# RWKV-7 recurrence with hashed experts: earlier loads for tiles 4 to 7, and the rounds of decays moved between two inversions

## The chip, the cores and the metric

The kernel runs on one core of one Trainium2 chip. The metric is the device time of one execution in microseconds (us), the median of several runs. The kernel before takes 647.45 us (three runs, 645.55 to 648.0); its profiled execution has a span of 645.1 us, and all times in the profile count from the start of that span.

The engines are named as the profile names them: PE is TensorE (matmul), PEld its weight loads, DVE is VectorE, ACT is ScalarE, POOL is GpSimd, SP is SyncE. SPq and POOLq are the queues of those two engines as issuers of DMA transfers.

## What is computed

Two blocks follow each other. The first is a recurrence with a state of 40 x 40 for each of 4 x 8 heads, over 768 steps; the second sends each of its 3072 output rows through one of 8 experts, chosen by a hash.

```python
# r, k, v, w, a, b: (4, 8, 768, 40)
for t in range(S):
    y[:, :, t] = einsum('bhd,bhde->bhe', rt, state)
    Sa = einsum('bhde,bhe->bhd', state, at)
    state = state * wt[:, :, None, :] - einsum('bhd,bhe->bhde', Sa, bt)
    state = state + einsum('bhd,bhe->bhde', vt, kt)
...
expert_idx = token_ids * 2654435761 % 8
for e in range(E):                       # x = y as rows (3072, 320)
    h = maximum(x[mask] @ w1[e], 0)
    out[mask] = h @ w2[e]
```

The kernel turns the recurrence into chunks of 64 steps. The products of the decays w over a chunk, called p and q, are multiplied into a, b, k and the output, so that within a chunk only matrices of 64 x 64 remain: one triangular matrix per head has to be inverted, and everything else is matmuls. Tile u is one chunk of two of the four batches (16 heads): 24 tiles in all.

## The kernel before

The kernel's instructions are not written in the order in which they run. Each piece of work registers itself with a "tick", and all pieces are recorded in the order of their ticks. Every engine then works through its own instructions strictly in that order. `order` settles ties. Tile u has its first part (scores) near tick u and its second part (the state's step) near tick u + 8. The names in STEPS give fractions of a tick.

```python
STEPS = ["r1","z","y","nc","x","at_t","x_t","s","u","sd","a","r_t","r0","rc"]

def at_tick(tick, step=None, order=0):
    if step is not None:
        tick += STEPS.index(step) / len(STEPS)
    ...                                  # plan.append((tick, order, n, f))
```

A "round" of decays makes p and q for two chunks, so for four tiles. It has three stages: five levels of products up a tree (`todo`), one matmul on PE that exchanges the halves' products (`f_ps`, from `own`), and two spreads down the tree that give p (in `pb`) and q (in `qb`).

```python
def decays(ri, t_w, t0, span, t_f, span_f=None, stores=None):
    @at_tick(t_w)                        # load w of the round into "wt"
    ...
    todo: 5 levels, pb and qb by DVE TENSOR_TENSOR (L368); the last is "own" (L365)
    then: 0  PE  f_ps <- own, partner                    (L384)
          1  DVE qb, ends <- f_ps, own                   (L391, L392)
          2  DVE reciprocal                              (L397)
          3  DVE pb spread, 4 levels                     (L377)
          4  DVE pb spread, last level; store p to DRAM  (L377, L339)
          5  DVE qb spread, 4 levels                     (L379)
          6  DVE qb spread, last level; store q to DRAM  (L379, L339)
          7  PE/ACT pend <- ends                         (L428, L433)
```

Round 0 is different: its p and q are turned into rows inside SBUF, and p's rows (`p_rows`) lie in a buffer of the tag "nu", which has one copy. They are written to DRAM as well, by one DMA (L408), since the output's multiplication needs them at tick 8.

```python
if ri == 0:
    x["p"] = p_rows = turned_rows(x["pb"][:],
        early.tile([P, 2*BLK*BLK], F32, tag="nu", name="p_rows"))
    at_tick_later.append(lambda: nc.sync.dma_start(pq_dram[ri][0]..., p_rows))   # L408
```

The same tag "nu" holds the working matrices of the inversion. One inversion serves a group of four tiles:

```python
def group_i(gi, t0, t1, t2):
    at t0 - 0.5:  nu = early.tile(..., tag="nu")           # POOL memset L591, L593
    at t0:        DVE transpose nu <- pk                   # L597
    t1 to t2:     30 steps of DVE multiply and add         # L615, L622
    at t2:        DVE transposes ut <- nu, twice           # L630, L631
...
for gi in range(NU // GRP):
    t0 = gi * GRP + GRP - 1 + t_a                          # t_a = 10/14
    group_i(gi, t0 + 0.05, t0 + 0.1, t0 + 3.4)
```

So group 0 takes its buffer at tick 3.26, is worked on from 3.76 and ends at 7.11; group 1 goes from 7.76 to 11.11, and so on. Between two inversions lie 0.65 ticks.

The inputs of a tile come by six DMAs from the SP queue (a, b and k, two halves each), into buffers `al` and `kb` of two copies each; for tiles 2 and 3 other buffers are lent (`x_t`, `mr`, `py`), which the second parts of the tiles need only from tick 8 on.

```python
@at_tick({0: -3.9, 1: -3.8, 2: -2.8, 3: -2.7}.get(u, max(u - 2.55, t_mult_of(u - 2) + 0.03)))
def _():
    kb_tag = {2: "x_t", 3: "mr"}.get(u)
    ...
    x["a"] = al = work.tile([P, DM], F32, tag="py" if kb_tag else "al", name="al")
    load(..., a, ...); load(..., b, ...); load(..., k, ...)          # L310

# DVE: at <- al, pl (L500) and z <- kb, ql (L507) at t_mult_of(u)
# PE: z_ps, t_ps, a_ps; ACT: z_t, at_t, pk, no; DVE: mk (L548)
```

`ql` and `pl` are q and p of the tile, loaded by the POOL queue (L468, L474). In the second part, PE runs in each tick r_ps, rc_ps, z_ps, y_ps, nc_ps, x_ps, t_ps, x_t_ps, s_ps, u_ps, sd_ps, a_ps; x_ps reads `ut` of the inversion, and u_ps needs both of its transposes.

Of the kernel before, what the change touches and what calls it, by code (L numbers as in the profile page):

```python
# [47 lines left out]
def kernel(  # L48
# [22 lines left out]
    NG = B // 2  # L71
# [100 lines left out]
# [4 lines that stand above are left out]
        def add(f):  # L176
            plan.append((round(tick, 4), order, len(plan), f))
            return f
        return add
# [53 lines left out]
    RN = P // (B * H * 2)  # L233
# [66 lines left out]
    def by_head(t, rows=slice(None)):  # L300
        return t[rows].rearrange("t (h e) -> t h e", h=H)
# [5 lines left out]
    def load(dst, src, b0, t0, crossed=False):  # L307

        for be in range(2):
            nc.sync.dma_start(dst(be, half(1 - be if crossed else be)),  # L310
                              src[b0 + be, :, t0:t0 + C, :].rearrange("h t e -> t h e"))
# [5 lines left out]
    def decays(ri, t_w, t0, span, t_f, span_f=None, stores=None):  # L317

        x = rounds[ri]
        todo, then = [], []  # L320
# [114 lines left out]
        if ri == 0:  # L435
            then = then[:3] + then[5:7] + then[3:5] + then[7:]
            at_tick_later = []
            at_tick(1.36)(lambda: [f() for f in at_tick_later])
        if stores is not None:
            at_tick(stores)(lambda: (store(0, x["pb"][:]), store(1, x["qb"][:])))  # L440
        for i, f in enumerate(todo):
            at_tick(t0 + span * i / len(todo), order=8)(f)
        for i, f in enumerate(then):
            at_tick(t_f[i] if isinstance(t_f, tuple) else t_f + span_f * i / len(then), order=8)(f)

    def of_batches(rows, b0, n):
        return rows[:, b0 * H:(b0 + n) * H, :].rearrange("t bh e -> t (bh e)")
# [3 lines left out]
    def t_mult_of(u):  # L451
        return u + LATE[u] - 0.1 if u in LATE else u - 0.6

    def tile_a(u):

        n, g = divmod(u, NG)
        ri, rn = divmod(n, RN)
# [6 lines left out]
        @at_tick({0: -2.2, 1: -2.19, 2: -0.9, 3: -0.8}.get(u, u - 1.7))  # L464
        def _():
            x["q"] = ql = work.tile([P, 2, DM], F32, tag="ql", name="ql")
            for be in range(2):
                nc.gpsimd.dma_start(ql[half(be)], of_batches(rows_of_chunk("q"), 2 * g, 2))  # L468
# [5 lines left out]
                nc.gpsimd.dma_start(pl[half(be)], of_batches(rows_of_chunk("p"), 2 * g + be, 1))  # L474


        @at_tick({0: -3.9, 1: -3.8, 2: -2.8, 3: -2.7}.get(u, max(u - 2.55, t_mult_of(u - 2) + 0.03)))
        def _():
            kb_tag = {2: "x_t", 3: "mr"}.get(u)
            if kb_tag:  # L480
                kb = work.tile([P, 2 * HP * P], F32, tag=kb_tag, name=f"kb_{kb_tag}", bufs=1)[:, 0:2 * DM].rearrange("p (b x) -> p b x", b=2)
            else:
                kb = work.tile([P, 2, DM], F32, tag="kb", name="kb")[:]
            x["kb"] = kb
            x["a"] = al = work.tile([P, DM], F32, tag="py" if kb_tag else "al", name="al")
            load(lambda be, rows: by_head(al, rows), a, 2 * g, n * C)

            load(lambda be, rows: by_head(kb[:, be], rows), b, 2 * g, n * C)
            load(lambda be, rows: by_head(kb[:, be], rows), k, 2 * g, n * C, crossed=True)
# [309 lines left out]
    t_a = STEPS.index("a") / len(STEPS)  # L799

    decays(0, -4.0, -3.0, 0.4, -2.5, 0.3)
    decays(1, -2.9, -1.9, 0.4, (-0.54, -0.53, -0.52, -0.5, -0.45, 0.75, 0.8, 0.85), stores=1.34)
    decays(2, 0.86, 2.7, 0.2, (3.0, 3.01, 3.02, 3.66, 3.67, 4.0, 4.3, 4.31))
    for ri in range(3, NR):
        t0 = ri * RN * NG - 5.0
        decays(ri, t0 - 2.0, t0 + 0.25, 1.0, t0 + 1.3, 1.1)
    for u in range(NU):
        tile_a(u)
        tile_s(u, u + LAG)
# [2 lines left out]
    for gi in range(NU // GRP):  # L812
        t0 = gi * GRP + GRP - 1 + t_a
# [500 lines left out]
```

## Time and profile before

| what | before |
|---|---|
| median of 3 runs | 647.45 us |
| span of the profiled execution | 645.1 us |
| first inversion, start of L597 to end of L631 | 46.98 to 88.82 us |
| recurrence with all engines, about | 89 to 396 us |
| experts, about | 396 to 645 us |
| PE / DVE / ACT / POOL busy, share of the span | 86% / 55% / 46% / 30% |
| DMA engines' busy share, 47 to 89 us | 0.96 |
| DMA engines' busy share, 131 to 280 us | 0.79 |

A line of a timeline gives the start, the duration (of several merged instructions where it ends in xN), the engine, the line of the kernel, the operation, and what it writes and reads. In brackets stand the engine's idle time just before it and what ended that. "issue" means that nothing in the profile explains the wait. A DMA instruction's own duration is that of its issue; the data land later.

### The profile page before, as it was taken

The page shows a single profiled execution, that of the slowest core. Times are in us where ns is not written, and L with a number is a line of the kernel's source. Part 1 is how long each engine was busy: PE and PEld are TensorE (multiplying, and loading weights), DVE is VectorE, ACT ScalarE, POOL GpSimd, SP SyncE. Part 2 cuts the span into 40 slices and gives each one's busy share as a digit, 9 for nine tenths or more (in the row PEclk, how much of TensorE's full clock was granted, in tenths as well). Part 3 has the DMA queues.
Part 4 walks back from the last instruction along what each step waited for, and adds up shares of the span by engine and source line. Part 5 has one row for each costly group of instructions (what it writes and reads, how often), then busy time and mean ns, then how long its engine had stood idle before and what let it go on. Part 6 is the DMA issues. An engine that isn't in the chain of part 4 may idle for free.

```text
span 645.1 us, 22962 instructions
## 1 busy us (share of the span) xinstructions
PE 556.3 (86%) x9866; PEld 422.7 (66%) x9866; DVE 351.6 (55%) x920; ACT 293.7 (46%) x695; POOL 195.8 (30%) x331
## 2 busy tenths in 40 slices
PE   0443568988999999999899998999999999999995
PEld 0332457877787878888788887666565646565552
DVE  6968679966977896797798553232021202203010
ACT  4162436757776677777767661113131304101100
POOL 0631341535333344432423321261313131230101
PEclk9975559989999999999999999999999999999999
DMA  8999988987797687842434613697333373220000
GB/s 160 198 197 178 163 154 143 190 144 137 149 184 148 129 169 149 153 97 45 103 60 116 155 53 97 223 290 248 110 102 113 105 264 103 66 96 20 30 12 25
DMA packets 195770, 85.13 MB, mean 132 GB/s; under 512 B 176718, under 2 KB 186191, under 8 KB 195664
## 3 DMA queue, kind: packets, MB, share of 16 engines
q1 hardware_dynamic: 184016, 45.59, 37.6%
q0 software_dynamic: 11456, 37.37, 20.1%
q8 instruction: 78, 1.28, 0.9%
q10 hardware_dynamic: 192, 0.66, 0.4%
q14 instruction: 28, 0.23, 0.1%
HBM read 66.54 MB, written 15.40 MB: 127 GB/s over the span
## 4 chain that ended last, share of the span: by engine, by line
PE 50%; issue 23%; DVE 10%; DMA 6%; SPq 5%; POOL 4%; ACT 2%; POOLq 0%; DVEq 0%; ACTq 0%
PE up_ps L1057 6%; PE dn_ps L1075 6%; PE y_ps L291 5%; PE s_ps L291 4%; PE rc_ps L291 3%; PE r_ps L291 3%; SPq L310 3%; PE x_t_ps L733 3%; PE a_ps L291 3%; PE t_ps L573 3%; PE sd_ps L793 3%; PE z_ps L521 2%; POOL out_dram L1080 2%; DVE mr L745 2%; PE nc_ps L291 2%
## 5 line engine op out<-in xcount | busy, mean ns | idle before, releaser
L1065 DVE TENSOR_SCALAR ht<-up_ps 128x416 f32<-128x416 f32 (+2 forms) x36 | 19.4, 543 | 165.2 <-PE up_ps L1062 163.7
L1075 PE MATMUL dn_ps<-w,ht 128*128 128x320 f32 x336 | 91.7, 433 | 0.0
L1057 PE MATMUL up_ps<-xt,w 128*128 128x416 f32 x224 | 81.3, 516 | 0.0
L1075 PEld LDWEIGHTS dn_ps<-w,ht 128*128 128x128 f32 x336 | 63.3, 190 | 25.5
L1080 POOL DMA_INDIRECT out_dram<-o,idx_all x26 | 26.1, 1004 | 165.4 <-ACT o L1079 164.3
L785 POOL DMA_DIRECT2D x_rows<-xs x44 | 23.2, 535 | 171.3 <-DVE xs L781 96.5
L1067 ACT ACTIVATE ht<-up_ps 128x416 f32<-128x416 f32 (+2 forms) x36 | 17.2, 478 | 107.5 <-PE up_ps L1062 107.4
L1057 PEld LDWEIGHTS up_ps<-xt,w 128*128 128x128 f32 x224 | 41.9, 190 | 36.8 <-issue 31.7
L615 DVE TENSOR_TENSOR outer<-nu 128x252 f32<-128x252 f32 (+8 forms) x180 | 63.4, 352 | 4.9
L622 DVE TENSOR_TENSOR nu<-nu,outer 128x252 f32<-128x252 f32 (+8 forms) x180 | 63.4, 352 | 4.3
L1079 ACT COPY o<-dn_ps 128x320 f32<-128x320 f32 x26 | 11.1, 425 | 92.4 <-PE dn_ps L1075 92.4
L521 PE MATMUL z_ps<-ident,z 128*104 128x128 f32 x192 | 31.2, 315 | 24.2 <-DVE z L507 21.4
L525 ACT COPY z_t<-z_ps 104x512 f32<-104x512 f32 x48 | 25.7, 588 | 47.4 <-PE z_ps L521 46.3
L521 PEld LDWEIGHTS z_ps<-ident,z 128*104 128x104 f32 x192 | 24.5, 150 | 27.1 <-issue 23.2
L468 POOL DMA_DIRECT2D ql<-q_rows x48 | 25.1, 531 | 48.4 <-DVE pb L377 15.4
L723 ACT COPY x<-nc_ps 64x320 f32<-64x320 f32 x48 | 20.1, 420 | 42.7 <-PE nc_ps L291 42.1
L745 DVE TENSOR_TENSOR mr<-rc_ps,after 128x1024 f32<-128x1024 f32 x24 | 29.3, 1220 | 13.6 <-PE rc_ps L291 13.6
L291 PE MATMUL rc_ps<-r_t,x_t 64*64 64x64 f32 x1536 | 30.1, 222 | 6.7 <-issue 6.0
L291 PE MATMUL a_ps<-at_t,z_t 64*64 64x64 f32 x1536 | 32.3, 241 | 3.6 <-ACT at_t L574 2.4
L291 PEld LDWEIGHTS a_ps<-at_t,z_t 64*64 64x64 f32 x1536 | 28.6, 152 | 8.1 <-ACT at_t L574 3.6
L548 DVE TENSOR_TENSOR mk<-a_ps,after 128x512 f32<-128x512 f32 x24 | 16.6, 690 | 28.9 <-ACT no L565 26.2
L291 PEld LDWEIGHTS rc_ps<-r_t,x_t 64*64 64x64 f32 x1536 | 25.7, 134 | 9.3 <-issue 6.1
(230 smaller groups left out, 1125.9 us busy)
## 6 DMA issues: line engine op xcount, KB each, us to landing
ql<-q_rows POOLq DMA_DIRECT2D x48, 160.0 KB, 4.3
w<-in_moe_w_dram SPq DMA_DIRECT2D x10, 640.0 KB, 7.6
w<-in_moe_w_dram SPq DMA_DIRECT2D x10, 512.0 KB, 4.3
al<-in_a_dram SPq DMA_DIRECT2D x48, 80.0 KB, 4.2
pl<-p_rows POOLq DMA_DIRECT2D x48, 80.0 KB, 4.5
r<-in_r_dram SPq DMA_DIRECT2D x48, 80.0 KB, 3.8
x<-in_v_dram SPq DMA_DIRECT2D x48, 80.0 KB, 3.7
py<-p_rows POOLq DMA_DIRECT2D x48, 80.0 KB, 4.8
```

Source lines behind the costliest of these rows:

```text
L291: nc.tensor.matmul(out_, lhsT=lhsT, rhs=rhs, start=start, stop=stop, skip_group_check=True)
L468: nc.gpsimd.dma_start(ql[half(be)], of_batches(rows_of_chunk("q"), 2 * g, 2))
L521: nc.tensor.transpose(p[0:R, be, hp * P:(hp + 1) * P], x["z"][:, be, hp, :], ident[:])
L525: nc.scalar.copy(t[0:R, be].rearrange("p h t -> p (h t)"), p[0:R, be])
L615: nc.vector.tensor_tensor(tv, paired(x["u"])[:, 0:full[1], j:j + 1, :].to_broadcast(full), paired(x["n"])[:, j // 2, j + 1:, j % 2].unsque ...
L622: nc.vector.tensor_tensor(o, o, x["t"][:, 0:n].rearrange("p (c i k) -> p c i k", c=full[1], k=2), op=OP.add)
L723: nc.scalar.copy(x["x"][half(be), be].rearrange("p (a q) (two e) -> p a (q two) e", a=2, two=2)[:, :, :, 0:D], p[half(be), :, 0:HP * D].re ...
L745: nc.vector.tensor_tensor(t[:].rearrange("p two h t -> p (two h) t"), p[:].rearrange("p two (h t) -> p (two h) t", t=C), after[:].unsqueez ...
L785: dma(x_of[2 * g + be, n * C:(n + 1) * C], xs[half(be), :])
L1057: nc.tensor.matmul(p[:], lhsT=w1[c][:, (f0 + i) * P:(f0 + i + 1) * P], rhs=xt[:, c, 0:n], start=(c == 0), stop=False)
L1075: nc.tensor.matmul(p[i * m:(i + 1) * m], lhsT=ht[:, f, c0:c0 + m], rhs=w2[f // (FP // 2)][:, f % (FP // 2), :], start=(f == 0), stop=(f == ...
L1080: st = nc.gpsimd.indirect_dma_start(out=out[:], out_offset=bass.IndirectOffsetOnAxis(ap=idx, axis=0), in_=o[0:m], in_offset=None, bounds_c ...
```

## The change

It does two things. The loads of tiles 4 to 7 get fixed, earlier ticks; tiles 6 and 7 borrow the buffers that tiles 2 and 3 had, so that they need not wait until tiles 4 and 5 have been used up. So that these loads come ahead of it, the DMA that writes round 0's p to DRAM is moved from tick 1.36 to 3.2. And rounds 3 to 5 of the decays, which before ran beside an inversion (round 3: products at ticks 7.25 to 8.25, the rest at 8.3 to 9.4), are put between two inversions (7.1 to 7.65), so that the inversion has VectorE for itself.

```diff
         if ri == 0:
             then = then[:3] + then[5:7] + then[3:5] + then[7:]
             at_tick_later = []
-            at_tick(1.36)(lambda: [f() for f in at_tick_later])
+            at_tick(3.2)(lambda: [f() for f in at_tick_later])
...
-            at_tick(t_f[i] if isinstance(t_f, tuple) else t_f + span_f * i / len(then), order=8)(f)
+            at_tick(t_f + span_f * i / len(then) if span_f else t_f[i], order=8)(f)
...
-        @at_tick({0: -3.9, 1: -3.8, 2: -2.8, 3: -2.7}.get(u, max(u - 2.55, t_mult_of(u - 2) + 0.03)))
-        def _():
-            kb_tag = {2: "x_t", 3: "mr"}.get(u)
+        @at_tick({0: -3.9, 1: -3.8, 2: -2.8, 3: -2.7, 4: 0.9, 5: 1.5, 6: 2.0, 7: 2.5}.get(u, max(u - 2.55, t_mult_of(u - 2) + 0.03)))
+        def _():
+            kb_tag = {2: "x_t", 3: "mr", 6: "x_t", 7: "mr"}.get(u)
...
     for ri in range(3, NR):
-        t0 = ri * RN * NG - 5.0
-        decays(ri, t0 - 2.0, t0 + 0.25, 1.0, t0 + 1.3, 1.1)
+        t0 = ri * RN * NG - 4.9
+        decays(ri, t0 - 2.1, t0, 0.12, [t0 + f for f in (0.13, 0.2, 0.21, 0.25, 0.35, 0.42, 0.5, 0.55)])
```

Before, the loads of tiles 4, 5, 6 and 7 stood at ticks 1.45, 2.45, 4.38 and 5.23. No arithmetic is added or removed.

## The prediction

> **What bounds the kernel now.** I read the busy table by stretches first. Up to 89 us PE is less than half busy (17.4 of the 42 us from 47 to 89) while DVE has 33.0 of 42 and the DMA engines a share of 0.96; from 131 to 280 us PE has 136.8 of 149. So the start is set by DVE and DMA, the recurrence by PE, and the change touches both. The experts after 396 us have nothing to do with it and only shift.
>
> Then the order in which the SP queue issues, because the change is mostly about that order:
>
> ```profile
> 19.04 1.99 SPq L310 DMA_DIRECT2D kb_mr<-in_k_dram  x2
> 30.11 4.20 SPq L339 DMA_DIRECT2D p_rows<-pb  x4
> 34.71 4.63 SPq L339 DMA_DIRECT2D q_rows<-qb  x4
> 39.39 1.71 SPq L408 DMA_DIRECT2D p_rows<-p_rows  x1
> 41.15 1.67 SPq L310 DMA_DIRECT2D al<-in_a_dram  x2
> ...
> 50.28 1.57 SPq L310 DMA_DIRECT2D kb<-in_k_dram  x2
> ```
>
> The queue stands still from 21.0 to 30.1 us behind the stores of round 1. The write of round 0's p (L408) follows the stores at once, and tiles 4 and 5 come only then (41.15 to 51.85 us).
>
> Who needs L408 is seen on POOL, and what follows on DVE:
>
> ```profile
> 44.63 0.95 POOL L591 MEMSET nu<- 128x1024 f32 x1 [1.22 <-DMA p_rows<-p_rows]
> ```
>
> ```profile
> 46.98 1.25 DVE L597 STREAM_TRANSPOSE nu<-pk 128x1024 f32<-128x1024 f32 x1 [1.21 <-ACT pk L564]
> ...
> 78.85 0.49 DVE L500 SCALAR_TENSOR_TENSOR at<-al,pl 128x320 f32<-128x320 f32 x1 [3.26 <-DMA al<-in_a_dram]
> 81.31 0.83 DVE L507 TENSOR_TENSOR z<-kb,ql 128x640 f32<-128x640 f32 x1 [1.97 <-DMA kb<-in_k_dram]
> ...
> 86.45 1.25 DVE L630 STREAM_TRANSPOSE ut<-nu 128x1024 f32<-128x1024 f32 x1
> 87.62 1.20 DVE L631 STREAM_TRANSPOSE ut<-nu 128x1024 f32<-128x1024 f32 x1
> ```
>
> The inversion cannot take the "nu" buffer before L408 has read round 0's p out of it: it landed 5.24 us after its issue (44.63 - 39.39). Here that just does not matter, as L597 waits until 46.98 for something else. From there DVE runs to 88.82 with 6.9 us idle in all: 5.23 us for the inputs of tile 7 (the two lines in the middle; this is what the change is after) and 1.66 us in two waits for ACT.
>
> PE's lines show what waits for the transposes, and the recurrence's gaps:
>
> ```profile
> 87.75 1.06 PE L291 MATMUL x_ps<-ut,no 32*32 32x32 f32 x32 [3.54 <-DVE ut L630]
> ...
> 90.61 1.06 PE L291 MATMUL u_ps<-um,xi 32*32 32x32 f32 x32 [0.75 <-ACT um L652]
> ...
> 136.05 0.45 PE L291 MATMUL rc_ps<-r_t,x_t 64*64 64x64 f32 x11 [2.26 <-issue]
> ```
>
> From 88 to 270 us PE waits only 1.8 us for DVE (twice y_ps for mr: 1.0 and 0.8), but 12.7 us for "issue". These gaps come once in about 380 matmuls, at places where the work has no boundary, such as after 53 of 64 rc_ps matmuls. No DVE work that moves away can remove them.
>
> **What the Trainium skill says.** "DMA: Bandwidth & Descriptors", Issuing engines are not separate DMA queues: transfers of all issuers run on the same 16 engines and interleave. The trace agrees: SP is idle from 21 to 30 us, yet the DMA share is 0.95 there, from POOL's transfers and the backlog. "Perfetto Trace Analysis", DMA Instruction — HWDGE: a DMA's reported window ends when its issue ends, the movement is outside. So L408's 1.71 us are not its cost; the 5.24 us until the memset are. "TensorE: Matmul & The Clock Gate", What's actually happening: after an idle window of about 3.4 us the array falls to half clock. The trace has half clock from 50 to 90 us, and after the 2.26 us gap above the next z_ps takes 1.95 us where it takes 1.08 in other ticks: PE waits that I add may cost more than their length. "Runtime: NRT & Kernel Launch", Instruction fetch mechanics: each engine's instructions are refilled in blocks of 256 by DMA and mostly hidden. 380 matmuls with their weight loads are 760 instructions, about three blocks, so I take the "issue" gaps for refills that the loaded DMA engines delay; the profile only suggests this, and here they are not hidden.
>
> **The change, part by part.** (1) The first inversion's start. In the changed program's SP order, tile 4's loads come before round 1's stores; tiles 5, 6, 7 follow the stores, and L408 only after them. Tile 4's buffers come free when DVE has done `at` of tile 0 (25.95 + 0.5), so its six loads go into the idle stretch: at the 0.67 us each that 12.25 to 16.28 shows for six, 26.5 to 30.5 us. Stores: 9.2 us as now (30.11 to 39.34), to 39.7. Eighteen loads: twelve took 8.8 us at 12.25 to 21.03 (0.73 each) and 10.7 us at 41.15 to 51.85 (0.89 each), so 13.2 to 16.0 us; I take 14.6, to 54.3. L408 lands 5.24 us later, at 59.5. L597 writes the same buffer and waits for the same DMA, so it starts near 59.5 instead of 46.98: +12.5 us. In DVE's order nothing of tiles 4 to 7 is ahead of L597, so DVE cannot fill that time.
>
> (2) From L597 on. The 5.23 us of waits for inputs vanish: -5.2. The first two products of round 3 (0.48 us each, 0.8 together by their starts) now stand ahead of L630: +0.8. L631 so ends at 88.8 + 12.5 - 5.2 + 0.8 = 96.9 instead of 88.8: **+8.1 us**.
>
> (3) Round 3 at the first x_ps. In the new PE order f_ps (from `own`) stands ahead of x_ps. DVE must first finish both transposes, then six products and `own` (0.32 + 0.32, 0.24 + 0.23, 0.19 + 0.19, 0.19; about 1.5 us by starts). f_ps takes 0.65, so x_ps begins about 2.2 us after L631. Before, u_ps began 1.8 us after L631; now x_ps 1.06, xi 0.74 and um 0.95 must come in between, so 4.9 us: **+3.1 us**.
>
> (4) Rounds 4 and 5, ticks 11.2 and 15.2: the same order, f_ps ahead of x_ps. From the end of rc_ps PE has r_ps 0.7, z_ps 1.0, y_ps 1.75, nc_ps 0.6 = 4.05 us until it wants f_ps. DVE has from there: mr 1.2, three steps 0.65, two products 0.8, two transposes 2.4, xs 0.4, the other products and `own` 1.25 = 6.7 us. PE waits 2.65 us in each round where it waited for nothing before: **+5.3 us**, or less where an "issue" gap falls into the same stretch.
>
> (5) What is given back: DVE no longer has 6 us of decays inside an inversion, so at most the two waits for mr, **-1.8 us**; the delayed start lets SP get ahead, so loads in front of the recurrence (the 5.25 us wait for ql at 90.95) meet less traffic: about **-1**; and gaps that coincide with (4): about **-1**.
>
> Sum: 8.1 + 3.1 + 5.3 - 1.8 - 2 = 12.7 us; 647.45 + 12.7 = 660. Two terms ((3) and (4)) rest on chains that may have slack which I do not see, so I put it at 659.
>
> **Rivals.** *A: the loads win.* If L408 lands early, the start is only freed of its waits: -5.2 us, and with the relief of DVE about -7, so 640 to 643. For it: DVE's 5.2 us are real. Against it: L408 stands behind 18 loads in one queue, and even at the quickest rate seen (0.65 us a load) it is issued at 51.4 and lands at 56.7, still 9.7 us late. *B: the DVE crowding is hidden.* If PE has other work before f_ps, (3) and (4) vanish: 651 to 652. Against it is the fixed order of PE. *C: crowding is worse.* If the longer waits drop PE's clock each time, 2 to 3 us more for each of three rounds, and the stores of p and q, now back to back (about 9 us of issue), delay instruction refills: 666 to 670.
>
> **Range and chances.** B's lower end gives 650, C's upper 669. The sum lies near the 2% border (660.4), so I split there: faster by over 2% 0.03, within 2% 0.52, slower by over 2% 0.45.
>
> **What will show it.** L408 issued at 53 to 56 us and the memset of "nu" waiting for it; L597 near 59 (step 1); no DVE wait for al or kb between L597 and L631, and L631 ending near 97 (2); x_ps waiting for f_ps, and f_ps for `own`, at the first tick (3) and in the ticks of rounds 4 and 5 with about 2.6 us (4); "issue" gaps of about 12.7 us in sum as now (5). I am wrong if L597 starts before 52 us, or if PE does not wait at f_ps.

## The result

The changed kernel takes 665.12 us (median of 4 runs, 663.02 to 667.51) against 647.73 us before: the ratio is 1.0274, with a 95% interval of 1.023 to 1.0319, so it is slower by 17.4 us. A second comparison, made later beside other kernels, gave 1.028 (1.0217 to 1.0342).

The profiled execution has a span of 662.8 us (645.1 before). The lines that answer to those of before follow. First the SP queue's timeline of the changed kernel:

```profile
29.53 1.33 SPq L310 DMA_DIRECT2D kb<-in_k_dram  x2
30.96 7.03 SPq L339 DMA_DIRECT2D p_rows<-pb  x4
38.09 5.00 SPq L339 DMA_DIRECT2D q_rows<-qb  x4
43.13 1.79 SPq L310 DMA_DIRECT2D al<-in_a_dram  x2
...
55.13 1.31 SPq L310 DMA_DIRECT2D kb_mr<-in_k_dram  x2
56.48 0.62 SPq L408 DMA_DIRECT2D p_rows<-p_rows  x1
```

Tile 4's loads went into the idle stretch, but the stores behind them took 12.1 us of issue instead of 9.2. Eighteen loads then took 13.35 us, and L408 came 17.1 us later than before. POOL's timeline shows who stands behind it, and VectorE's shows the inversion:

```profile
60.30 0.95 POOL L591 MEMSET nu<- 128x1024 f32 x1 [13.11 <-DMA p_rows<-p_rows]
```

```profile
60.28 1.25 DVE L597 STREAM_TRANSPOSE nu<-pk 128x1024 f32<-128x1024 f32 x1 [13.98 <-DMA p_rows<-p_rows]
...
74.96 0.69 DVE L548 TENSOR_TENSOR mk<-a_ps,after 128x512 f32<-128x512 f32 x1 [1.08 <-ACT no L565]
...
84.46 0.69 DVE L548 TENSOR_TENSOR mk<-a_ps,after 128x512 f32<-128x512 f32 x1 [0.59 <-ACT no L565]
...
93.94 0.69 DVE L548 TENSOR_TENSOR mk<-a_ps,after 128x512 f32<-128x512 f32 x1 [1.08 <-ACT no L565]
95.45 0.49 DVE L368 TENSOR_TENSOR pb<-wt 128x320 f32<-128x320 f32 x1
95.86 0.48 DVE L368 TENSOR_TENSOR qb<-wt 128x320 f32<-128x320 f32 x1
96.26 1.24 DVE L630 STREAM_TRANSPOSE ut<-nu 128x1024 f32<-128x1024 f32 x1
97.42 1.20 DVE L631 STREAM_TRANSPOSE ut<-nu 128x1024 f32<-128x1024 f32 x1
```

Both POOL and DVE wait for the same DMA, DVE for 14 us. After it no wait for al or kb is left, as intended; three short waits for ACT remain. On PE, the waits of more than a microsecond for other engines that are new, and the first u_ps, whose short wait is as before:

```profile
100.13 0.65 PE L384 MATMUL f_ps<-own,partner 128*128 128x40 f32 x2 [5.96 <-DVE own L365]
...
103.57 1.06 PE L291 MATMUL u_ps<-um,xi 32*32 32x32 f32 x32 [0.75 <-ACT um L652]
...
111.88 0.68 PE L291 MATMUL nc_ps<-r,um 64*64 64x40 f32 x32 [1.16 <-ACT z_t L525]
...
155.84 0.42 PE L384 MATMUL f_ps<-own,partner 128*128 128x40 f32 x2 [2.84 <-DVE own L365]
...
214.67 0.56 PE L384 MATMUL f_ps<-own,partner 128*128 128x40 f32 x2 [3.10 <-DVE own L365]
```

The start of s_ps, which runs once in every tile, serves as a milestone. Its shift against the profile of before shows where the time went:

| landmark | before, us | changed, us | shift, us |
|---|---|---|---|
| first L597 starts | 46.98 | 60.28 | +13.3 |
| first L631 ends | 88.82 | 98.62 | +9.8 |
| first u_ps starts | 90.61 | 103.57 | +13.0 |
| s_ps of tile 0 | 100.37 | 114.47 | +14.1 |
| s_ps of tile 2 | 127.55 | 140.83 | +13.3 |
| s_ps of tile 3 (round 4 just ahead) | 143.90 | 159.43 | +15.5 |
| s_ps of tile 6 | 185.87 | 200.66 | +14.8 |
| s_ps of tile 7 (round 5 just ahead) | 199.25 | 218.77 | +19.5 |
| s_ps of tile 11 | 254.57 | 271.74 | +17.2 |
| s_ps of tile 21 | 370.29 | 387.95 | +17.7 |

The start lost 14.1 us, the intervals up to tile 3 and up to tile 7 lost 2.25 and 4.73 us (16.35 to 18.60 and 13.38 to 18.11), and the rest gave back 3.4 us.

### The profile page after: what moved, and what is told of

It reads as the page before. It is cut to its first block, busy times and chain, and to the rows that moved or that the text cites. A ratio compares the mean times of both kernels' runs of the same rounds, so it can differ in the third digit from the quotient of the medians.

```text
span 662.8 us, 22963 instructions
## 1 busy us (share of the span) xinstructions
PE 560.6 (85%) x9866; PEld 425.8 (64%) x9866; DVE 355.0 (54%) x920; ACT 294.1 (44%) x695; POOL 195.9 (30%) x331
## 3 DMA queue, kind: packets, MB, share of 16 engines
q8 instruction: 78, 1.28, 0.8%
## 4 chain that ended last, share of the span: by engine, by line
PE 47%; issue 21%; DVE 12%; SPq 6%; DMA 5%; POOL 4%; ACT 3%; POOLq 0%; DVEq 0%; ACTq 0%
PE up_ps L1058 6%; PE dn_ps L1076 6%; PE s_ps L291 4%; PE y_ps L291 4%; SPq L310 4%; PE x_t_ps L733 3%; PE a_ps L291 3%; PE t_ps L573 3%; PE rc_ps L291 3%; PE r_ps L291 3%; DVE mr L745 3%; POOL out_dram L1081 2%; PE sd_ps L793 2%; PE x_ps L291 2%; SPq L339 2%
## 5 line engine op out<-in xcount | busy, mean ns | idle before, releaser
L1068 ACT ACTIVATE ht<-up_ps 128x416 f32<-128x416 f32 (+2 forms) x36 | 17.2, 478 | 107.5 <-PE up_ps L1063 107.4
L384 PE MATMUL f_ps<-own,partner 128*128 128x40 f32 x12 | 3.3, 373 | 37.7 <-DVE own L365 37.7
```

## The experiments

Two theories for the loss stood from the prediction. Theory P: the place of L408 in the SP queue delays the inversion. Theory F: f_ps, ahead of x_ps in PE's order, makes PE wait for VectorE. The rivals were that the early loads themselves cost the start, and that VectorE's crowding between the inversions holds PE up wherever f_ps stands. All ratios are against runs of the kernel before made alongside in the same comparison. Between comparisons the median of the kernel before moved from 644.7 to 649.1 us, so only ratios are compared.

| version | L408 at tick | loads | rounds 3 to 5 | ratio | 95% interval |
|---|---|---|---|---|---|
| changed | 3.2 | early | between | 1.0274 | 1.023 to 1.0319 |
| e1 | 1.36 | early | between | 1.0123 | 1.0035 to 1.021 |
| e2 | 3.2 | early | as before | 1.0136 | 1.0063 to 1.0208 |
| e3 | 1.36 | as before | between | 1.0125 | 1.0028 to 1.0223 |
| e4 | 3.2 | early | between, f_ps late | 1.0155 | 1.0072 to 1.0237 |
| e5 | 3.2 | as before | as before | 1.0 | 0.9979 to 1.002 |
| m1 | 1.36 | early | between, f_ps late | 0.9979 | 0.9953 to 1.0005 |
| m2 | 1.36 | early | as before | 0.9981 | 0.9961 to 1.0 |
| d1 | 2.25 | early | as before | 1.0119 | 1.0053 to 1.0185 |
| m3 | 1.2 | early | as before | 0.9944 | 0.9916 to 0.9971 |

### e1: the write ahead of the loads of tiles 5 to 7

```diff
-            at_tick(3.2)(lambda: [f() for f in at_tick_later])
+            at_tick(1.36)(lambda: [f() for f in at_tick_later])
```

> The changed kernel with one edit: the write of round 0's p (L408) back at tick 1.36, directly behind round 1's stores and ahead of the loads of tiles 5 to 7. Theory P (the place of L408 in the queue costs the start): L408 is issued near 43 us, lands near 48.5, L597 starts there instead of at 60.3, everything after it is 11 to 12 us earlier: 653 us. Rival L (the early loads themselves cost the start, by their traffic and by slowing round 1's stores from 9.2 to 12.1 us): L597 gains little for the end, 660 or more.

Ratio 1.0123: 1.5% less than the changed kernel, about 10 us where 12 were expected. From VectorE's timeline of this run:

```profile
47.98 1.25 DVE L597 STREAM_TRANSPOSE nu<-pk 128x1024 f32<-128x1024 f32 x1 [1.74 <-DMA p_rows<-p_rows]
...
84.31 1.20 DVE L631 STREAM_TRANSPOSE ut<-nu 128x1024 f32<-128x1024 f32 x1
```

L597 is back by 12.3 us with all loads still early, and the inversion ends 3.3 us before that of the old kernel. So the place of L408 costs the start, and the early loads by themselves do not. The stores of round 1 took 11.5 us of issue here too, so their slowness was not what hurt: with them L597 is 1.0 us later than before.

### e2 and e3: each part of the change alone

e2 is the changed kernel with the rounds of decays put back:

```diff
-        t0 = ri * RN * NG - 4.9
-        decays(ri, t0 - 2.1, t0, 0.12, [t0 + f for f in (0.13, 0.2, 0.21, 0.25, 0.35, 0.42, 0.5, 0.55)])
+        t0 = ri * RN * NG - 5.0
+        decays(ri, t0 - 2.0, t0 + 0.25, 1.0, t0 + 1.3, 1.1)
```

> The changed kernel with the rounds of decays 3 to 5 where they were before; loads and L408 as changed. Theory P plus F (f_ps ahead of x_ps makes PE wait in three rounds): only the start is late, L631 near 97.8, no PE wait at f_ps, first s_ps 9 us later than before, 656 to 657 us. Rival L2 (all of the loss is in the loads' part): 661 or more. Rival D (all of it is in the decays' part): 648 to 650.

e3 is the kernel before with this hunk reversed, so with the new decays alone.

> The kernel before with only the rounds of decays 3 to 5 moved between two inversions. Theory F: PE waits at f_ps before the first x_ps (start later by 4 to 5 us), and in the ticks of rounds 4 and 5 by about 3 us each, with half clock after it (7 us for both), 3.5 us given back elsewhere: 655 to 656 us. Rival D0 (moving the decays off the inversion pays, the loss is all in the loads): 645 or less.

The ratios are 1.0136 and 1.0125; together 2.6%, which is the whole loss within the intervals. Neither part pays alone. In e2 the first s_ps came at 108.5 us (expected: 9 us late; it was 8.1) and PE did not wait at f_ps in rounds 4 and 5. In e3 the list of PE's waits, 80 to 280 us, begins thus:

```profile
PE f_ps L384 <- DVE own L365: 13.4, 3, 6.8
```

Three waits, 13.4 us in sum (6.80, 2.84 and 3.72): theory F. The first takes the place of a wait for the transposes that was 3.5 us before, so some 9.9 us are new; the ratio is worth 8.1 us. Not each of them reaches the end in full: the first s_ps came at 102.34 us, only 2.0 us late where 4 to 5 were expected, while the tick of round 5, from s_ps to s_ps, took 18.21 us (13.38 before).

### e4: f_ps behind s_ps

```diff
-        decays(ri, t0 - 2.1, t0, 0.12, [t0 + f for f in (0.13, 0.2, 0.21, 0.25, 0.35, 0.42, 0.5, 0.55)])
+        decays(ri, t0 - 2.1, t0, 0.12, [t0 + f for f in (0.41, 0.42, 0.43, 0.44, 0.46, 0.5, 0.54, 0.6)])
```

> The changed kernel with the matmul f_ps and what follows it later: PE comes to f_ps after s_ps (in the first tick after x_ps), not ahead of x_ps; VectorE's products stay between the inversions, the rest follows behind the state's update. Theory F: no wait of PE at f_ps beyond 0.5 us, no half clock in those ticks, 10 to 11 us less than the changed kernel: 654 to 655. Rival C (VectorE's crowding between the inversions holds PE up wherever f_ps stands): PE waits as long for ut, st or mk, 662 or more.

Ratio 1.0155: 1.2% less than the changed kernel, about 7.7 us where 10 to 11 were expected. PE's timeline in the tick of round 4:

```profile
148.89 0.69 PE L291 MATMUL x_ps<-ut,no 32*32 32x32 f32 x32
149.52 0.65 PE L573 MATMUL t_ps<-ident,at 128*128 128x128 f32 x4
150.01 1.04 PE L733 MATMUL x_t_ps<-ident,x 128*128 128x128 f32 x8
150.88 0.70 PE L291 MATMUL s_ps<-st,ident 104*104 104x320 f32 x2
151.51 0.81 PE L291 MATMUL s_ps<-x,z 128*40 128x40 f32 x32
152.26 0.41 PE L384 MATMUL f_ps<-own,partner 128*128 128x40 f32 x2
```

No wait in brackets, and x_t_ps at full clock. The ticks of rounds 4 and 5 took 13.88 and 13.28 us from s_ps to s_ps, where the changed kernel took 18.60 and 18.11, and e4's first s_ps came 5.6 us earlier than that kernel's; the two ratios alone hardly tell the versions apart, as their intervals touch. The products up the tree stand where they did; f_ps and the vector work that follows it stand later, still between the same inversions. That this later work adds nothing to the gain isn't shown apart, but the wait that went is one for `own`, which is ahead of it. A little crowding is left: in the first tick and in that of round 5, x_ps waits for the transposes (4.27 us, 3.54 before, and 0.42 us); two products of the round still stand ahead of them.

### e5: the late write alone, which failed to cost anything

The kernel before with L408 at tick 3.2.

> The kernel before with one edit: L408 at tick 3.2, so that it stands behind the loads of tiles 4 and 5 (12 of them) where it stood ahead. Theory P: those took 10.7 us, so L408 is issued near 50, lands near 55, L597 starts there, 8 us late, and all of it reaches the end: 1.2 to 1.3% slower than before. Rival L (early loads, not the write, delay the start): within 0.4% of before.

This expectation was wrong: the ratio is 1.0 (0.9979 to 1.002). The SP queue and VectorE of this run:

```profile
48.99 0.62 SPq L408 DMA_DIRECT2D p_rows<-p_rows  x1
```

```profile
52.77 1.25 DVE L597 STREAM_TRANSPOSE nu<-pk 128x1024 f32<-128x1024 f32 x1 [6.68 <-DMA p_rows<-p_rows]
...
81.30 0.48 DVE L500 SCALAR_TENSOR_TENSOR at<-al,pl 128x320 f32<-128x320 f32 x1
81.70 0.82 DVE L507 TENSOR_TENSOR z<-kb,ql 128x640 f32<-128x640 f32 x1
...
89.18 1.20 DVE L631 STREAM_TRANSPOSE ut<-nu 128x1024 f32<-128x1024 f32 x1
```

L597 was late as theory P says, though by 5.4 us and not 8, against an unchanged kernel profiled beside it (47.33). But its last transpose ended only 1.6 us later (90.38 against 88.82). The inversion used to stand still for tile 7's inputs at `at` and `z` (4.9 us in that profile); starting later, it found them there, and only a wait for ACT of 1.1 us came out in their place. My expectation had counted the delay and left out the wait that it removes, though step 2 of the prediction has just that term. So the late write alone costs nothing that can be measured: it eats the very slack that the early loads were made to remove. The first s_ps still came 2.0 us later (102.42 us), which is 0.3%, just more than the interval allows at the end; what gives it back isn't shown.

For that baseline the kernel before was profiled again:

> The kernel before, unchanged, for landmarks from the same chip as the three next to it: first L597 near 47, end of L631 near 88.8, first s_ps near 100 us.

It gave L597 at 47.33, L631 ending at 88.82 and the first s_ps at 100.38, in a span of 640.8 us. The start is the same to 0.4 us; the 4.3 us to the first profile of before came later, in the recurrence, where the waits named "issue" differ from run to run (98 to 270 us: 12.7 us then, 10.3 here).

### d1: the write in the middle, with the early loads

e2 with L408 at tick 2.25, behind the loads of tiles 4 to 6.

```diff
-            at_tick(3.2)(lambda: [f() for f in at_tick_later])
+            at_tick(2.25)(lambda: [f() for f in at_tick_later])
```

> Loads as changed, decays as before, L408 at tick 2.25: behind the loads of tiles 4, 5 and 6, so 6 fewer ahead of it than in the changed kernel and 12 more than where L408 follows round 1's stores directly. Theory P with slack (a late write first eats up VectorE's later waits for inputs; with the early loads there are none left, so each us passes through): L408 lands near 54.5 to 55.5, L597 there, end of L631 near 91.5 to 92.5 (84.8 with the write first, 96.5 with it last), 0.8 to 1.0% slower than before if the start's 7 us pass on in full, 0.4% if half is absorbed later. Rival S (a threshold: VectorE has slack of its own): L631 below 88.

Ratio 1.0119. VectorE's timeline:

```profile
55.90 1.25 DVE L597 STREAM_TRANSPOSE nu<-pk 128x1024 f32<-128x1024 f32 x1 [9.39 <-DMA p_rows<-p_rows]
...
91.64 1.20 DVE L631 STREAM_TRANSPOSE ut<-nu 128x1024 f32<-128x1024 f32 x1
```

With the loads early and the decays as before, three places of L408 now line up: L597 at 47.98, 55.90 and 59.72 us gives L631 starting at 83.59, 91.64 and 95.33 us, 35.6 to 35.7 us later each time. Nothing is absorbed any more: each microsecond that L408 is late passes through VectorE, and on to PE, where the first s_ps comes at 96.18, 104.02 and 108.48 us.

### m1, m2, m3: the parts put together

m1 is the changed kernel with the edits of e1 and e4, m2 with those of e1 and e2, m3 is m2 with L408 at tick 1.2, ahead of round 1's stores.

> The changed kernel with both edits: L408 at tick 1.36 and f_ps late. Theories P and F: the start is 3 to 4 us earlier than before (the waits for tile 7's inputs are gone, part of it lost to round 3's products ahead of the transposes), no wait at f_ps; 0 to 0.6% faster than before. Rival C (crowding between inversions): 0.5% slower or more.

> The loads of tiles 4 to 7 as changed, L408 at tick 1.36, rounds 3 to 5 of decays as before: only the first part of the change, without the late write. Theory P: L597 near 48, L631 ends 3.5 to 4 us earlier than before, nothing lost later: 0.4 to 0.7% faster than before. Rival L (earlier loads bring nothing since transfers are bound by the 16 engines): the same as before within 0.2%.

> As the version with only the loads moved and the write first, but L408 at tick 1.2, between tile 4's loads and round 1's stores. Theory P: L597 no longer waits for L408 (near 47.2 instead of 47.98), so at most 0.8 us earlier: 0.2 to 0.5% faster than before. Rival Q (the stores of round 1, pushed back by the write, delay ql and pl of tiles 4 and 5): the same as before or slower.

m1 and m2 come out alike, 0.9979 and 0.9981, both within or at the edge of no difference. They differ only in the place of the decays: once f_ps no longer stands in PE's way, moving them off the inversion brings nothing that can be measured here, as little as PE waited for VectorE in the recurrence before (1.7 us, for mr). m2's start is 4.2 us ahead of the unchanged kernel's (first s_ps at 96.18 against 100.38), but its ratio shows 0.2% and not the 0.4 to 0.7% expected; why the rest does not reach the end isn't shown. m3 is the only version whose interval stays clear of 1: ratio 0.9944 (0.9916 to 0.9971), 0.6% in one comparison.

```profile
30.77 0.62 SPq L408 DMA_DIRECT2D p_rows<-p_rows  x1
31.49 8.02 SPq L339 DMA_DIRECT2D p_rows<-pb  x4
```

```profile
47.43 1.25 DVE L597 STREAM_TRANSPOSE nu<-pk 128x1024 f32<-128x1024 f32 x1 [1.22 <-ACT pk L564]
...
83.61 1.20 DVE L631 STREAM_TRANSPOSE ut<-nu 128x1024 f32<-128x1024 f32 x1
```

L597 again waits for ACT and not for the write. Its inversion ends at the same time as m2's, so the profile does not explain a lower time than m2's; the intervals of the two overlap, so that they differ at all isn't shown.

### The changed kernel once more

> The changed kernel, unchanged, for the same chip: 2.3 to 3.0% slower than before; f_ps waits of 6, 2.8 and 3.1 us.

1.028, with waits at f_ps of 5.98, 1.28 and 3.71 us: the second was shorter than expected. PE had then already stood still for "issue" (1.89 us at 152.00, in the same tick), as step 4 of the prediction allowed.

## Why the prediction was right, and where it was too small

The forecast was 659 us with a range of 650 to 669; 665.12 lies inside. The chances were nearly even between "within 2%" (0.52) and "slower by over 2%" (0.45); it became the second, the one given a little less. The mechanisms held, but the loss was 17.4 us where 11.5 were forecast, half as much again; it is inside the range because the range reached up to rival C. Four sizes were too small.

**Step 1** said L408 issued at 54.3 and L597 at 59.5, so +12.5 us. Measured: 56.48 and 60.28, +13.3. That the two are so near is partly luck, as errors nearly cancelled: the stores took 12.1 us instead of 9.2, but the eighteen loads 13.4 instead of 14.6, and L408 landed (from its issue to the start of the memset) in 3.8 us, not 5.24. The prediction had carried over a landing measured right behind the stores to a place behind loads: in the six profiles where L408 follows the stores directly it took 5.1 to 5.3 us, in the six where it follows loads 3.8 to 4.0. e1, which takes only this delay away and keeps the early loads, is 1.5% faster.

**Step 2** took 5.2 us off for the vanished waits. Those waits did vanish, but a wait for ACT of 1.08 us at the last mk (93.94) that had been hidden behind them came out, so VectorE's idle time fell from 6.9 to 2.75 us, by 4.1. The 0.8 us for two products ahead of the transposes was exact (95.45 to 96.26). L631: +9.8 instead of +8.1.

**Step 3** said +3.1 us at u_ps. Measured from the end of L631: 4.95 us instead of 1.79, +3.16. What it left out is one more wait: nc_ps stood 1.16 us for z_t of ACT. Up to the first s_ps the start lost 14.1 us where steps 1 to 3 have 11.2.

**Step 4** said 2.65 us of wait in each of rounds 4 and 5. Measured: 2.84 and 3.10. But the two intervals grew by 7.0 us and not by 5.3, since PE fell to half clock after the wait, which I had put into rival C. The tick of round 5, before and changed:

```profile
196.66 0.68 PE L291 MATMUL nc_ps<-r,um 64*64 64x40 f32 x32
...
198.38 1.04 PE L733 MATMUL x_t_ps<-ident,x 128*128 128x128 f32 x8
199.25 0.70 PE L291 MATMUL s_ps<-st,ident 104*104 104x320 f32 x2
```

```profile
210.89 0.68 PE L291 MATMUL nc_ps<-r,um 64*64 64x40 f32 x32
...
217.06 1.92 PE L733 MATMUL x_t_ps<-ident,x 128*128 128x128 f32 x8
218.77 1.27 PE L291 MATMUL s_ps<-st,ident 104*104 104x320 f32 x2
```

From nc_ps to s_ps it went from 2.59 to 7.88 us, in the tick of round 4 from 2.60 to 7.10. Of these 9.8 us, 5.9 are the waits and 0.8 f_ps itself; x_ps, t_ps and x_t_ps took 1.25 us longer in round 4 and 1.62 in round 5. The milestones show 7.0 and not 9.8 chiefly because before had an "issue" gap of 2.26 us, with half clock after it, in one of the two intervals. The windows of the changed kernel around round 5 (columns: stretch, its length, busy time of PE, PEld, DVE, ACT and POOL with their instructions, granted clock, DMA share, GB/s):

```profile
208.00:212.00 4.00, 3.24 (x87) 2.73 (x85) 3.93 (x9) 1.59 (x4) 0.00 (x0) 1.00 0.47 75
212.00:216.00 4.00, 1.33 (x34) 1.26 (x34) 3.21 (x12) 0.53 (x2) 1.71 (x3) 0.85 0.15 37
216.00:220.00 4.00, 4.00 (x26) 3.03 (x20) 3.32 (x8) 3.26 (x7) 3.52 (x8) 0.50 0.51 135
```

This agrees with what the prediction drew from the Trainium skill ("TensorE: Matmul & The Clock Gate", What's actually happening): the clock falls after idle time. The size does not agree: the page gives an idle window of about 3.4 us, but here the clock fell after idle pieces of 3.10 and 2.84 us, and before after one of 2.26. What was measured decides.

**Step 5** expected 3.8 us given back; it was 3.4. Which share belongs to which of its terms isn't shown. PE's wait for mr went only from 1.7 to 1.0 us; the "issue" gaps, which I had expected to stay at 12.7 us, summed to 6.9 us between 98 and 280 us. They also differ between two profiles of the same kernel: in the four profiles in which PE waits at f_ps (the changed kernel twice, e1, e3) they sum to about 5 to 8 us, in the others to 7.5 to 13, so some of them may have fallen into those waits. m1 against m2 shows that the relief of VectorE is worth nothing measurable. That these gaps are refills of instructions was argued only; no run here tests it.

**The rivals.** A (the loads win) was wrong for the change as made, and its -5.2 us was near what the loads can do: e1 and m2 end the inversion 3.3 and 4.0 us earlier than before, once the write stands ahead. B (PE has other work before f_ps) fell by all three waits, and e4 shows what it takes to make it true. C (half clock) holds for part of the excess.

The sum of the steps was 12.7 us, and I took about one off for slack that I did not see. That was the wrong direction: the three things left out of the sum (an ACT wait coming out, an ACT wait behind the first tick, half clock) all added.

## What to carry to other kernels

When transfers are moved ahead in one queue, ask what they now stand in front of, and who holds a buffer for it: here 18 loads made a 0.6 us write hold the buffer of the next stage for 13 us. A delay and an earlier arrival can use the same slack: the late write alone cost nothing measurable, the early loads alone (m2) gained 4 us at the start, together (e2) they lost 8 there, so such parts have to be measured together and alone. And where work moves on one engine, look for the single instruction by which another engine waits for it; here the place of one 0.4 us matmul decided about 1.2% of the time.

## What was not expected of the hardware

A wait of 2.84 or 3.10 us on PE cost more than its length, here by 1.25 and 1.62 us in x_ps, t_ps and x_t_ps behind it, most of which ran at half clock. Which idle piece is long enough is not a matter of its length alone: in the profile of before the clock fell after a gap of 2.26 us and not after one of 2.03 (the next z_ps took 1.95 and 1.08 us), but in e1 it fell after a gap of 1.57 (z_ps 1.71 us).

The issue of the same four p stores took 4.0 to 4.2 us with an idle queue ahead of them, 6.4 to 7.3 us with six loads just ahead, and 8.0 us with the 640 KB write ahead too, so an issue's duration went with what was issued just before it. The 640 KB write itself landed 5.1 to 5.3 us after its issue behind the stores and 3.8 to 4.0 behind loads. Its own issue did not decide that: in e3 it took 0.64 us, in before 1.71, and the landing 5.31 and 5.24.

And two profiles of one kernel differed by 4.3 us of span, with the start the same to 0.4 us.
